# Transposing rows by DMA in a two-block spectral and attention network

## The chip, the cores and the metric

The kernel runs on one core of a Trainium2 chip. The core has a matrix engine (PE; its weight loads are shown as PEld), a vector engine (DVE), a scalar engine (ACT), a general engine (POOL) and a queue engine (SP) that issues most of the DMA transfers. The engines run their own instruction lists in order and wait for each other by semaphores. The metric is the device time of one execution in microseconds (us).

## The reference

x has 2048 rows of 512 columns in bfloat16. Four steps follow each other, each adding to x: a spectral layer, an attention layer, and both once more with the same weights.

```python
x = A_x
x = x + _A_ref(_layernorm(x, axis=-1), A_w_r, A_w_i)
x = x + _B_ref(_layernorm(x, axis=-1), B_wq, B_wk, B_wv, B_wo)
x = x + _A_ref(_layernorm(x, axis=-1), A_w_r, A_w_i)
x = x + _B_ref(_layernorm(x, axis=-1), B_wq, B_wk, B_wv, B_wo)

def _A_ref(x, w_r, w_i):          # 2-D real FFT over rows and columns, a filter, and back
    X = jnp.fft.rfft2(x.astype(jnp.float32), axes=(-2, -1)) * (w_r + 1j * w_i)
    return jnp.fft.irfft2(X, s=(S, D), axes=(-2, -1)).astype(jnp.bfloat16)

def _B_ref(x, wq, wk, wv, wo):    # 32 heads of 16; all heads share one k and one v
    q, k, v = heads(x @ wq), x @ wk, x @ wv
    p = softmax(einsum("bhqd,bkd->bhqk", q, k) * 16 ** -0.5)
    return merge(einsum("bhqk,bkd->bhqd", p, v)) @ wo
```

## The kernel before, in words

x lies in SBUF as 16 tiles of 128 rows by 512 columns (`tile_of(x_sb, k)`); `xn_sb` holds the normed rows in the same form. A matrix product on PE needs the operand that is summed over along the partitions, so x (for the spectral layer) and the normed rows (for queries, keys and values) are also kept transposed: `xT` and `xTa`, each [128, 4, 16, 128], four blocks of 128 columns for each of 16 tiles. `transpose_pair` (L191) makes two tiles of them: eight PE transposes against an identity into one bank of PSUM, and one copy to SBUF, by ACT (L198) or DVE (L200).

The spectral layer (`spectral_layer`, L210) has these stages:

- The first pass, ten steps k: transpose tiles 2k and 2k+1 of x (L195); one step later `forward` multiplies them with a cosine and sine table (L254) and ACT scales the result by the row's norm (L181); another step later `first` (L205 to L207, copied at L268) begins the transform over rows and writes to DRAM, from where `cross1` reads it in another order. Nine more steps do the same for the other half of the frequencies. `load` places the weight loads (wr_sb, wi_sb, 1 MB each) at fixed steps of the pass.
- The middle: `filtered` and `back`, with another exchange through DRAM.
- The last pass, nine steps q: `along` (L355), `last` (L368 to L370), ACT copies the sums to x (L389), DVE takes the row statistics (L152). At q = 3, 5 and 7 `norm.shift` norms tiles 0-3, 4-7 and 8-11 (two of four on ACT, L172, two on DVE, L174). At q = 4 and 6 `att.turn` transposes tiles 0-3 and 4-7 of the normed rows, and at q = 5 and 7 `att.keys_values` makes keys and values of them (L426, L452). Six idle matmuls (LASTW, L401) end the layer.

In the spectral layer the order on PE, ACT, DVE and SP is the order in the source. In attention that holds for PE and DVE; the source order is made while the kernel is built, by a planner (`Clock`, and the loop in `attention_layer`) that keeps its own account of when each engine is free. The attention layer (`attention_layer`, L589) consists of steps n. In each, PE makes a pair of score tiles (sc, L876) and ACT takes their exponential (L1042). Beside it, DVE makes a bit-arithmetic exponential of other score tiles (aux, L876, then L916, L948, and L940 on POOL), in three phases. PE multiplies both kinds with the values (L831). When there is nothing else, PE multiplies zeros (L846). Between the steps the planner places jobs: transposes of the normed tiles (`job_turn`, L621), keys and values of tiles 8-11 and 12-15, queries, and the output projection (`job_out`, L654), which adds to x (L659). A job has a first step at which it may run and a step at which it has to (`TURN` for tiles 12-15). `DVE0` is the planner's time at which DVE is free for attention's work. The transposes of tiles 8-15 (four `job_turn`) are such jobs, and the norm of tiles 12-15 is queued on DVE after the second of them.

The last four tiles' output projection of the first attention layer is left to the next spectral layer: `rest` (L1115, added to x at L1117) runs in steps k = 2 and 3 of its first pass. Large buffers come from a pool of six (`bigp`, tag "big"); a new one waits until the buffer's last reader is done.

## Time and profile before

| | us |
|---|---|
| median of 3 runs | 1414.54 (1411.57 to 1414.83) |
| the profiled execution's own time | 1409.2 |
| its span | 1407.4 |
| first spectral layer | about 0 to 92 |
| first attention layer, exponentials | 93.0 to 704 |
| second spectral layer | about 705 to 791 |
| second attention layer, exponentials | 791 to 1399 |
| ACT, exponentials (L1042), busy in all | 1218.0 |
| PE / DVE / ACT / POOL busy | 1355.2 / 1312.6 / 1337.0 / 818.2 |

Times in the profile's views are counted from the start of the span. A busy engine is not always the one that others wait for: the chain of waits follows the work that ended last back to what released it, and the rows by window tell which engine has no gap in a stage. A time in a chain row is the share of that piece in the chain, which can be shorter than the instruction.

### The profile page before, as it was taken

Reading aid. Unit: us, or ns where it says so; the run is one execution under the profiler, and the core shown is the slowest. Engines: PE = TensorE matmul, PEld = TensorE weight load, DVE = VectorE, ACT = ScalarE, POOL = GpSimd, SP = SyncE. Lnnn points to the kernel's source line nnn. Section 1 sums busy time; section 2 is a strip of 40 time slices with the busy share of each in tenths; the row PEclk is TensorE's granted clock in tenths of the full one; section 3 lists DMA queues with packets and bytes.
Section 4 is the critical chain, followed back from the end, with each engine's and each line's share of the span. In section 5 each row is a group of like instructions: output and inputs, shape, how many; then the busy total and the mean of one; then the engine's idle time right before and its main releaser. Section 6 shows DMA issues by size and latency. Waiting matters only on the chain.

```text
span 1407.4 us, 34962 instructions
## 1 busy us (share of the span) xinstructions
PE 1355.2 (96%) x14166; PEld 473.3 (34%) x14166; DVE 1312.6 (93%) x2274; ACT 1337.0 (95%) x1551; POOL 818.2 (58%) x477
## 2 busy tenths in 40 slices
PE   8899999999999999999997999999999999999998
PEld 6642232222222222222275422322222222222222
DVE  5679999999999999999966899999999999999997
ACT  6689999999999999999956899999999999999997
POOL 2115676667666667667600166666666666666665
PEclk9999999999999999999999999999999999999999
DMA  8700000000000000000064000000000000000000
GB/s 261 221 7 2 2 2 2 1 2 1 2 2 2 2 2 2 2 1 2 2 186 145 1 1 2 1 2 9 5 5 2 6 9 5 2 1 9 9 2 16
DMA packets 38242, 32.94 MB, mean 23 GB/s; under 512 B 3520, under 2 KB 35520, under 8 KB 37568
## 3 DMA queue, kind: packets, MB, share of 16 engines
q1 hardware_dynamic: 35104, 27.40, 6.7%
q8 instruction: 110, 1.80, 0.6%
q0 software_dynamic: 576, 2.10, 0.4%
q10 hardware_dynamic: 2400, 1.21, 0.3%
q14 instruction: 52, 0.43, 0.1%
HBM read 20.22 MB, written 10.49 MB: 22 GB/s over the span
## 4 chain that ended last, share of the span: by engine, by line
ACT 49%; PE 33%; issue 8%; DVE 6%; DMA 2%; POOL 0%; SPq 0%; DVEq 0%; ACTq 0%
ACT e L1042 47%; PE pv L831 13%; PE sc L876 11%; DVE ph L916 2%; PE aux L876 2%; PE ps L254 2%; DVE ln_stats L152 1%; PE aux L426 1%; PE ps L205 1%; PE aux L654 1%; PE pv L846 1%; DMA tab_C<-const_C 1%; DVE ph L948 1%; DMA B<-D 1%; PE ps L355 1%
## 5 line engine op out<-in xcount | busy, mean ns | idle before, releaser
L1042 ACT ACTIVATE e<-sc 128x1024 bf16<-128x1024 f32 x1328 | 1218.0, 1175 | 1.9 <-PE sc L876 1.9
L940 POOL TENSOR_TENSOR ph<-ph,step 128x1024 int32<-128x1024 int32 x404 | 763.2, 1892 | 410.3 <-DVE ph L948 284.3
L916 DVE TENSOR_SCALAR ph<-aux 128x512 uint16<-128x512 f32 x1440 | 903.3, 678 | 19.9 <-PE aux L876 15.8
L831 PE MATMUL pv<-ph,vaug 128*32 128x512 bf16 x4320 | 548.8, 386 | 0.6 <-POOL ph L940 0.3
L876 PE MATMUL sc<-QT,Kv 32*128 32x512 bf16 x2656 | 522.0, 380 | 19.1 <-ACT e L1042 13.9
L831 PE MATMUL pv<-e,vaug 128*32 128x512 bf16 x2656 | 483.9, 384 | 0.3 <-ACT e L1042 0.3
L876 PE MATMUL aux<-QT,Kv 32*128 32x512 bf16 x1440 | 455.9, 384 | 0.0
L876 PEld LDWEIGHTS <-Kv 32*128 32x128 bf16 x4096 | 183.0, 91 | 525.9 <-issue 517.8
L846 PE MATMUL pv<-wo_sb,zeros 128*32 128x512 bf16 x1200 | 257.8, 383 | 0.0
L831 PEld LDWEIGHTS <-vaug 128*32 128x32 bf16 x6976 | 147.5, 94 | 292.6 <-issue 281.6
L948 DVE TENSOR_SCALAR ph<-ph 128x2048 uint16<-128x2048 uint16 x316 | 216.1, 684 | 0.5
L158 POOL TENSOR_TENSOR ln_rstd<-ln_veps,mhalf 128x4 f32<-128x4 f32 x16 | 16.6, 1036 | 140.1 <-DVE ln_veps L157 140.0
L152 DVE BATCH_NORM_STATS2 ln_stats<-x_sb 128x6 f32<-128x512 bf16 x64 | 43.4, 678 | 22.1 <-ACT x_sb L389 16.3
L846 PEld LDWEIGHTS <-zeros 128*32 128x32 bf16 x1200 | 60.2, 94 | 1.9 <-issue 0.3
L746 DVE STREAM_TRANSPOSE oT<-pv 128x512 f32<-128x512 f32 x64 | 45.1, 705 | 9.2 <-PE pv L831 9.2
L181 ACT ACTIVATE Pk<-ps,ln_rstd 128x256 bf16<-128x256 f32 x64 | 27.1, 478 | 15.9 <-PE ps L254 15.6
L426 PE MATMUL aux<-xTa,wq_sb 128*128 128x512 bf16 x120 | 39.5, 385 | 0.4 <-DVE ph L916 0.2
L254 PE MATMUL ps<-tab_PH,xT 128*128 128x256 bf16 x256 | 35.5, 286 | 1.6 <-DVE xT L200 1.0
L268 DVE CAST A<-ps 128x512 bf16<-128x512 f32 x28 | 19.3, 690 | 18.8 <-PE ps L207 18.8
L654 PE MATMUL aux<-wo_sb,ph 128*128 128x512 bf16 x96 | 31.8, 384 | 1.5 <-DVE ph L916 1.0
L768 POOL TENSOR_TENSOR on<-oT,rden 128x512 bf16<-128x512 f32 x30 | 31.7, 1058 | 2.0 <-DVE rden L772 1.8
L254 PEld LDWEIGHTS <-xT 128*128 128x128 bf16 x256 | 24.8, 102 | 5.5 <-DVE xT L200 1.3
(108 smaller groups left out, 677.9 us busy)
## 6 DMA issues: line engine op xcount, KB each, us to landing
D<-A SPq DMA_DIRECT2D x32, 128.0 KB, 3.3
A<-D SPq DMA_DIRECT2D x16, 256.0 KB, 3.5
D<-B SPq DMA_DIRECT2D x32, 128.0 KB, 3.2
B<-D SPq DMA_DIRECT2D x12, 256.0 KB, 4.1
tab_H<-const_H POOLq DMA_DIRECT2D x4, 512.0 KB, 6.3
wr_sb<-in_A_w_r_dram SPq DMA_DIRECT2D x2, 1024.0 KB, 6.1
wi_sb<-in_A_w_i_dram SPq DMA_DIRECT2D x2, 1024.0 KB, 7.5
out_dram<-x_sb SPq DMA_DIRECT2D x15, 128.0 KB, 1.7
```

Of the source, the lines that this page charges most:

```text
L152: nc.vector.bn_stats(st, src)
L254: nc.tensor.matmul(ps[:, j, :], lhsT=xT[:, cc, 2 * k + j, :], rhs=PH[:, cc, 256 * h:256 * h + 256], start=(cc == 0), stop=(cc == NC - 1), ...
L426: self.nc.tensor.matmul(ps, lhsT=w(c), rhs=self.xTq[:, c, qc * 512:(qc + 1) * 512], start=(c == 0), stop=(c == NC - 1), skip_group_check=True)
L654: nc.tensor.matmul(ps, lhsT=OTs[qb][:, g4, kk * P:(kk + 1) * P], rhs=wo_sb[:, g4, :], start=first, stop=last, skip_group_check=True)
L746: end = clock.now(clock.FLIP, lambda: nc.vector.transpose(out=oT[:, par].rearrange("p b c -> p (b c)"), in_=pv), clock.last + clock.MM_END)
L831: nc.tensor.matmul(pv_tiles[gi][32 * i:32 * i + 32, :], lhsT=vaug[:, kc, j, :], rhs=es, start=((gi, i) not in started), stop=(left[gi, i] ...
L846: nc.tensor.matmul(pv_tiles[gi][32 * i:32 * i + 32, :], lhsT=att.zeros, rhs=wo_sb[:, 0, :], start=False, stop=False, skip_group_check=True)
L876: nc.tensor.matmul(out, lhsT=Kv[r, par, kc * P:(kc + 1) * P], rhs=QT[r, g, qb * 512:(qb + 1) * 512], start=True, stop=True, skip_group_che ...
L916: end = clock.now(clock.Z, lambda: nc.vector.tensor_scalar(out=z.bitcast(U16), in0=ps, scalar1=SCALE * LOG2E * 128.0, scalar2=127.0 * 128. ...
L940: nc.gpsimd.tensor_tensor(out=copy.bitcast(I32), in0=z.bitcast(I32), in1=step.to_broadcast([P, w // 2]), op=ALU.add)
L948: nc.vector.tensor_scalar(out=one.bitcast(U16), in0=z.bitcast(U16), scalar1=float(PHASE[1]), scalar2=None, op0=ALU.add)
L1042: nc.scalar.activation(out=e[:, 0:ng * 512], in_=sc[:, 0:ng, :].rearrange("p a b -> p (a b)"), func=ACT.Exp, scale=SCALE)
```

## The change: DMA transposes

A new function issues one DMA transpose on SP for one tile, SBUF to SBUF:

```diff
+def turn_tile(nc, rows, xT, k):
+    nc.sync.dma_start_transpose(out=xT[:, :, k, :], in_=tile_of(rows, k))
```

All 16 tiles of normed rows in both layers go through it. Tiles 0-11 are transposed in the spectral layer's last pass, each group of four right after its norm (q = 3, 5, 7). Tiles 12-15 are normed at the head of attention and transposed there. The four `job_turn` are gone.

```diff
@@ last pass of spectral_layer
             if 0 <= g < 3 and odd == 0:
                 norm.shift(4 * g, (1, 3))
-            if 0 <= g < 2 and odd == 1:
-                att.turn(psum, g, "pa")
+                att.turn(g)
@@ Attention.turn
-        for k2 in (2 * qc, 2 * qc + 1):
-            transpose_pair(self.nc, self.tabs["ident"], psum, self.xn_sb, self.xT, k2, k2 % 2 == 1, tag)
+        for k in range(4 * qc, 4 * qc + 4):
+            turn_tile(self.nc, self.xn_sb, self.xT, k)
@@ attention_layer
-        def job_turn(k2):
...
+        def turn_last():
+            for k in range(12, 16):
+                turn_tile(nc, att.xn_sb, att.xT, k)
+
+        clock.later(0.2, lambda: norm_in.bias(12))
+        for i in range(4):
+            clock.later(clock.one(2), lambda i=i: norm_in.one(12, i, False), True)
+        clock.later(0, turn_last)
+        while clock.queue:
+            clock.flush_one()
...
-        jobs = [(0, 0, job_turn(4)), (0, 0, job_turn(5)), (0, 0, job_keys(2)), (0, 0, job_values(2)),
-                (TURN, TURN, job_turn(6)), (TURN, TURN, job_turn(7)), (TURN, TURN, job_keys(3)), (TURN, TURN, job_values(3))]
+        jobs = [(0, 0, job_keys(2)), (0, 0, job_values(2)), (TURN, TURN, job_keys(3)), (TURN, TURN, job_values(3))]
@@ constants
-TURN, DVE0 = 7, 1.7
+TURN, DVE0 = 12, 2.4
```

For the second spectral layer, x is transposed during the first attention layer: once twelve tiles have their sums and the last queries are made, which frees the buffer of `xTa`, SP issues twelve transposes; the last four tiles follow in `rest`. The second layer's first pass has no PE transposes of x; the first layer's keeps them.

```diff
+        xT, summed = [], [0]
+
+        def turn_sums():
+            if store is None and summed[0] == 12 and ("Q", NQB - 1, 3) in made:
+                xT.append(att.bigp.tile([P, NC, 16, P], BF, name="xT", tag="big"))
+                for t in range(12):
+                    turn_tile(nc, x_sb, xT[0], t)
@@ spectral_layer
-        xT = bigp.tile([P, NC, 16, P], BF, name="xT", tag="big")
+        xT = feed.xT or bigp.tile([P, NC, 16, P], BF, name="xT", tag="big")
...
-            if k < 8:
+            if k < 8 and feed.xT is None:
                 transpose_pair(nc, tabs["ident"], psum, x_sb, xT, k, feed.busy or k % 2 == 1, "pa")
@@ rest
                 nc.vector.tensor_tensor(out=tile_of(x_sb, t), in0=ps, in1=tile_of(x_sb, t), op=ALU.add)
+                turn_tile(nc, x_sb, xT[0], t)
                 norm_out.stats(t, tile_of(x_sb, t))
```

More of the change, by code (lines that the diff above doesn't have):

```diff
@@ L429, in project, with turn @@
                 yield
-    def turn(self, psum, qc, tag):
+    def turn(self, qc):
         if qc == 0:
@@ L619, in job_queries @@
             made.add(("Q", qc, g))
-        def job_turn(k2):
-            while k2 > 5 and ("N", 3) not in made:
-                clock.flush_one()
-            ps = aux_tile((P, 2, NC, P), BF)
-            for tt in range(2):
-                for cc in range(NC):
-                    nc.tensor.transpose(ps[:, tt, cc, :], tile_of(att.xn_sb, 2 * k2 + tt)[:, cc * P:(cc + 1) * P],
-                                        att.tabs["ident"])
-                if tt == 0:
-                    yield
-            dst = att.xT[:, :, 2 * k2:2 * k2 + 2, :].rearrange("d c tt p -> d tt c p")
-            evict(clock.CAST, lambda: nc.vector.tensor_copy(out=dst, in_=ps))
-            if k2 == 5:
-                clock.later(0.2, lambda: norm_in.bias(12))
-                for i in range(4):
-                    clock.later(clock.one(2), lambda i=i: norm_in.one(12, i, False), True)
-                clock.later(0, lambda: made.add(("N", 3)))
+            turn_sums()
+        def turn_last():
[7 more added lines that the diff above has]
+            clock.flush_one()
         def job_keys(qc):
@@ L671, in job_out @@
                 return
+            summed[0] += 1
+            turn_sums()
             clock.later(0.96, lambda: norm_out.stats(k, tile_of(x_sb, k)))
@@ L1117, in rest @@
                 nc.vector.tensor_tensor(out=tile_of(x_sb, t), in0=ps, in1=tile_of(x_sb, t), op=ALU.add)
+                turn_tile(nc, x_sb, xT[0], t)
                 norm_out.stats(t, tile_of(x_sb, t))
-    rest.busy = False
+    rest.busy, rest.xT = False, xT[0]
     return rest
@@ L1185, in feed @@
             nc.vector.tensor_single_scalar(out=tabs["S1N"][:, part], in_=tabs["S1"][:, part], scalar=-1.0, op=ALU.mult)
-    feed.busy = True
+    feed.busy, feed.xT = True, None
     for layer in range(2):
```

## Prediction

> **What bounds the kernel now.** I read the page's totals first, then a table of windows, the chain of waits around the stages that the change touches, and the DMA rows.

> Window table (start:end, length, then busy us and instruction count of PE, PEld, DVE, ACT, POOL; granted clock, DMA share, GB/s):
> ```profile
> 84.00:91.00 7.00, 7.00 (x62) 4.04 (x61) 4.93 (x13) 5.14 (x9) 1.01 (x1) 1.00 0.00 0
> 96.00:106.00 10.00, 9.77 (x107) 4.23 (x105) 9.96 (x22) 9.75 (x11) 1.89 (x1) 1.00 0.00 0
> 200.00:300.00 100.00, 98.28 (x1043) 29.55 (x1039) 96.81 (x164) 100.00 (x110) 67.27 (x37) 1.00 0.01 2
> 721.00:736.00 15.00, 14.76 (x158) 13.14 (x156) 7.72 (x12) 9.73 (x23) 0.00 (x0) 1.00 0.89 226
> ```
> In attention ACT does nothing but the exponentials (L1042), is busy 100.00 of 100 us, and starts 109 in 100 us (one per 0.917; the count takes in one at an edge). Its rows in part 5 show 1.9 us of idle time before all 1328. So attention lasts 664 x 0.917 us after its first exponential: fewer PE or DVE instructions there gain next to nothing, and an early wait of ACT is not made up. What can move is when attention's exponentials get going, and the spectral stages, where PE fills the windows (7.00 of 7.00; 14.76 of 15.00).

> The chain of waits (start, length, work), end of the first spectral stage and start of attention:
> ```profile
> 73.96 1.52 ACT xn_sb L172 x2
> ...
> 79.41 1.02 PE ps L426 x4
> ...
> 84.29 0.89 PE pst L195 x16
> ...
> 89.49 1.52 ACT xn_sb L172 x2
> ...
> 95.30 0.59 PE aux L426 x2
> 95.89 0.34 PE sc L876 x2
> 96.25 1.94 ACT e L1042 x2
> ```
> Rows 0 to 3 are normed at 73.9 to 75.5, their keys begin at 79.41; the last of rows 8 to 11 is ready at 91.0, their keys begin at 95.30. The exponentials began at 93.04, had a gap of 0.36, and never stop after 96.25.

> The same chain, start of the second spectral stage:
> ```profile
> 706.17 0.70 DVE xT L200
> 706.92 1.05 PE ps L254 x8
> 707.97 0.88 PE ps L1115 x4
> ...
> 717.71 1.05 PE ps L254 x8
> ...
> 719.20 0.45 PE pst L195 x8
> ```
> A group of eight PE transposes takes 0.45 of PE; twice PE waits for a copy of xT.

> DMA rows (KB each, median us from issue to landing) and SP's queue (start, length of the issue):
> ```profile
> D<-A SPq DMA_DIRECT2D x32, 128.0 KB, 3.3
> D<-B SPq DMA_DIRECT2D x32, 128.0 KB, 3.2
> wr_sb<-in_A_w_r_dram SPq DMA_DIRECT2D x2, 1024.0 KB, 6.1
> out_dram<-x_sb SPq DMA_DIRECT2D x15, 128.0 KB, 1.7
> ```
> ```profile
> 43.36 1.24 SPq L132 DMA_DIRECT2D tab_CS<-const_CS  x1
> 44.65 0.43 SPq L132 DMA_DIRECT2D tab_PSC<-const_PSC  x1
> ```

> **The price that no row shows.** A DMA transpose of one tile (128x512, 128 KB) is not in this trace. Two numbers matter: p, the time that SP holds for one issue, and L, from issue to landing. For p the ends are 0.43 (a plain issue) and 1.24 (the longest single one). For L they are 1.7 and 4.1 (B<-D, 256 KB). A transpose cuts the tile into 256-byte runs, twice as many as D<-A's 512-byte ones, so more must be set up than for a plain copy: I take p = 1.24, the upper end, and L = 3.2, the median of a plain 128 KB. All are on SP, one after another.

> **End of each spectral stage (twice).** Removed: 32 PE transposes in att.turn (two groups of 16, 0.89 each on PE), two ACT copies (1.02) and two DVE copies (0.69). Added: 12 DMA transposes on SP, behind plain loads that landed before (wq, wo issued by 65). Nothing else is on SP here.
> Rows 0 to 3: the first is ready at 74.3, so the fourth issue is at 74.3 + 3 x 1.24 = 78.0 and lands at 81.2. PE without its 0.89, and ACT without a copy of 1.02, would be at the keys by 78.4; instead it waits until about 81.25: 1.85 later than before, not 1.0 earlier. Behind that wait stand, in PE's order, the values, the first queries and all following sums.
> Rows 4 to 7: ready by about 81, landed by 87; their keys stand at 81.25 + (87.62 - 79.41 - 0.89) = 88.6. Hidden, with 1.5 us to spare.
> Rows 8 to 11: their norm hangs on the sums before the second keys. Before, the first came 2.2 after the start of these keys (87.62 to 89.8), so now 90.8. The fourth issue is at 90.8 + 3.72 = 94.5, landing 97.7. Before, PE transposed these rows inside attention, behind one pair of scores each; now the second thing PE does in attention, after the first pair, is the keys of rows 8 to 11. PE gets there at 88.6 + 1.27 (keys, values) + 2.15 (ten sums) + 1.3 (LASTW) + 0.3 = 93.6 and waits 4.1 us. The second pair of scores is queued behind. From keys to the next exponential it took 0.95 (95.30 to 96.25); now exponential 2 starts at 98.65, and the fourth, which was at 96.25, at 98.65 + 2 x 0.907 = 100.5. **Loss: 4.2 us per layer, 8.4 in all.**
> With both ends: at p = 0.43, L = 1.7 the keys start at 78.4 (PE and ACT decide), 85.7 and 91.0, and the same exponential at 93.75: a gain of 2.5 per layer. At p = 1.24, L = 4.1 it is a loss of 6.0.

> **Attention.** Four groups of 8 PE transposes and four DVE copies (0.68) per layer go; ACT is the bound, so zero, and it stays covered as ACT is at 100%. The norm of rows 12 to 15 (bias, four of 0.35) moves to DVE's head of attention, behind POOL's rstd (L158, 1.01). Queued behind it are the krep copy and all vector units; rstd comes about 96.8, the norm ends at 98.4, and the first copy behind it needs the keys of 97.7 and after: zero, and 1.5 us if rstd were late. Rows 12 to 15 are wanted at step 12 (TURN), about 98.65 + 11 x 0.917 - 1 = 107.7; their fourth lands by 97.4 + 3.72 + 3.2 = 104.3: zero, cover 3.4 us. The twelve transposes of x can begin when the last queries (651) and sums (637) of attention 1 are made and are wanted at 705: 12 x 1.24 + 3.2 = 18 of 53 us, zero. Exponentials, vector units and POOL copies stay 1328, 1440 and 404; zero-fillers on PE rise by 51, in gaps.

> **Start of the second spectral stage (once).** Removed: 64 PE transposes, four ACT copies, four DVE copies. The first copy (0.70 at 706.17) stands on DVE ahead of the OT transposes that the rest of the output projection (L1115) waits for: 0.85 earlier. Six groups inside the PE-filled loop: 6 x 0.45 = 2.7. The wait before 717.71: 0.56. Sum 4.1. Against it: rows 12 to 15 of x are added there (L1117) and transposed by SP. 12 and 13 go at once; 14 and 15 are issued after the 1 MB of wr_sb, issue near 712.1 and landing 6.1 later, 718.2; I put them at 719.2, and the forward step that reads them would start at 722.72 - 4.1 = 718.6: 0.6 lost. **Gain 3.5.** Ends: 4.4 (no such wait) and 2.0 (L = 4.1 and DMA, busy 0.89 until 736, giving some back); all later steps of that stage follow PE.

> **Sum.** 8.4 - 3.5 = +4.9 us on the profiled execution (1409.2 with a span of 1407.4): 1414.1. The runs shown have a median 5.3 above that execution, so 1414.54 + 4.9 = 1419.4. Range of this case: L = 2.2 with gain 3.5 gives +0.9 (2 x 2.2 - 3.5), L = 4.1 with gain 2.0 gives +10.

> [...] For a 128x128 transpose the row is 0.45 per eight on PE plus a copy of 0.68 for the pair of tiles. [...]

> **Rivals.**
> 1. Faster: an issue is as cheap as a plain one. Place: the fourth transpose before the keys of rows 0 to 3 and 8 to 11. p = 0.43 with L = 3.2 gives keys at 79.0, 86.3 and 93.1, a gain of 0.4 per layer, total -4.3 (1410.2); with L = 1.7, 2 x -2.5 and -4.4 give -9.4 (1405.1). For it: most issues of the trace take 0.43 to 0.5. Against: none of them transposes. At L = 3.2 it decides at p = 0.85, where the sum is zero.
> 2. Transfers do not overlap: each tile takes its 3.2 alone. Then the twelfth lands at 74.3 + 12 x 3.2 = 112.7, the keys of rows 8 to 11 are 17.4 later, exponentials 19 per layer: +38 - 2 = +36 (1450). Against: plain DMAs of 128 KB issue 0.5 apart and overlap in the rows. [...]
> 3. PE's clock falls in the wait of 4.1 us. Eight L254 matmuls took 1.91 at 14.47 and 1.04 at 17.22, so PE does start slow; after the gap of 2.17 before 745.00 it did not. At half pace a step of 0.917, 98% PE, takes about 1.8; four us so lose 2 per layer: +4.9 + 4 = +9 (1423). [...]

> **Chances.** Forecast 0.55; rival 1 0.24; rival 2 0.08; rival 3 0.13. Within 0.3% (4.2 us, about what a measurement can tell from no change): 0.25 of the forecast, as +0.9 to +4.2 lies in its range, and 0.05 of rival 1: 0.30. Faster 0.19, rounded to 0.20. Slower 0.50: 0.30 of the forecast and rivals 2 and 3. Eight in ten: from rival 1's lower end, 1405, to 1430 (rival 3 at L = 4.1: +10 + 4, and a margin of 1.5); rival 2 is left out.

> **What would show it.** SP rows of the transposes: length 1.24, landing 3.2. PE waits before the keys of about 2.8 and 4.1 us per layer, released by DMA. ACT idle of some 4 us after its first exponential, then one per 0.917. The forward step of x rows 14 and 15 some 3.5 earlier after the end of attention 1. Wrong: if p is below 0.85, if the keys wait for ACT or DVE rather than a DMA, or if exponentials run at another pace than 0.917.

## The result, and the profile after

The changed kernel takes 1430.43 us (median of 5 runs, 1428.15 to 1435.57); the kernel before took 1414.54 beside it (5 runs, 1411.57 to 1415.77). The ratio is 1.0122, 95% interval 1.0098 to 1.0146: slower by 16 us where +4.9 was forecast, with an upper end of 1430. The profiled execution of the changed kernel took 1435.57 (span 1433.8), the slowest of its five, and that of before 1409.2, its fastest, so the two traces lie 26.4 apart. 5.0 of that is there before any changed instruction has run: rows 0 to 3 are normed by 80.49 instead of 75.48 behind the same first passes. In the profiles of kernels whose first pass is the same, this point lies between 75.0 and 81.2. Losses are therefore counted from the end of that norm in each layer.

Windows of the profile after, for the stages that the prediction showed (columns as there):
```profile
84.00:91.00 7.00, 4.90 (x32) 2.53 (x34) 2.60 (x9) 3.28 (x5) 0.56 (x1) 0.76 0.57 77
103.00:113.00 10.00, 9.47 (x69) 2.19 (x69) 6.17 (x14) 6.86 (x7) 0.00 (x0) 0.57 0.27 54
200.00:300.00 100.00, 96.14 (x1042) 28.69 (x1043) 98.12 (x166) 100.00 (x111) 67.09 (x37) 1.00 0.01 1
726.00:741.00 15.00, 14.09 (x138) 11.74 (x136) 9.96 (x19) 7.57 (x19) 1.04 (x1) 1.00 0.82 187
```
The granted clock was 1.00 in all four stages before. It is 0.76 at the end of the spectral stage (its last pass, called the tail below) and 0.57 in the first steps of attention (called the head), where PE is busy 9.47 of 10 us but does 69 matmuls where it did 107 in the ten microseconds shown of before, and ACT is busy only 6.86. In the middle of attention nothing has changed: ACT is full.

The chain of waits there (start, length, work):
```profile
78.97 1.52 ACT xn_sb L172 x2
...
83.37 2.43 DMA xTa<-xn_sb
85.89 1.02 PE ps L429 x4
86.91 0.39 PE ps L455 x16
87.29 1.63 PE ps L429 x4
...
100.30 0.74 ACT e L1048
101.04 2.45 DMA xTa<-xn_sb
103.53 0.60 PE aux L429 x2
104.14 0.32 PE sc L882 x2
104.46 0.97 PE aux L429 x2
105.43 0.54 PE sc L882 x2
```
A transfer now stands ahead of the keys of rows 0 to 3 (85.89) and of rows 8 to 11 (103.53); PE waits 3.18 and 3.32 us for them, and ACT, behind the second, 3.17:
```profile
85.89 1.02 PE L429 MATMUL ps<-xTa,wka 128*128 128x512 bf16 x4 [3.18 <-DMA xTa<-xn_sb]
...
103.53 0.60 PE L429 MATMUL aux<-xTa,wka 128*128 128x512 bf16 x2 [3.32 <-DMA xTa<-xn_sb]
```
```profile
104.50 1.02 ACT L1048 ACTIVATE e<-sc 128x1024 bf16<-128x1024 f32 x1 [3.17 <-PE sc L882]
```
In the second layer PE waits 3.20 and 3.71 and ACT 4.19. Behind both waits the same work takes longer: the four projections of the queries 1.63 (0.88 in the chain before, at 80.82), a pair of scores 0.54 (0.34 before, at 95.89).

The DMA rows (KB where given, median us to landing) and the transposes in the tile's rows (length of the issue in ns, least, median, most):
```profile
xTa<-xn_sb SPq DMA_TRANSPOSE x32, 2.4
xT<-x_sb SPq DMA_TRANSPOSE x16, 2.5
```
```profile
L204 SPq DMA_TRANSPOSE xTa<-xn_sb x16: 1190/1218/1639, 79.4 to 107.2; - x16
```
So p is 1.22 and L 2.4.

SP's queue at the start of the second spectral stage:
```profile
727.96 0.58 SPq L235 DMA_DIRECT2D wr_sb<-in_A_w_r_dram  x1
728.64 4.34 SPq L204 DMA_TRANSPOSE xT<-x_sb  x2
```
The last two tiles of x stand behind the 1 MB load, as forecast. The first of their two issues took 3.03 and landed 6.19 after its start; the second took 1.22, as usual, and the rest of the 4.34 is a pause between them.

And a gap that the forecast had not: near the 257th exponential of the first layer, PE's and DVE's rows show
```profile
339.95 1.21 DVE L157 TENSOR_SCALAR ln_veps<-ln_mv 128x4 f32<-128x4 f32 x1
```
```profile
341.80 0.40 PE L837 MATMUL pv<-ph,vaug 128*32 128x512 bf16 x4 [0.89 <-DVE ph L922]
```
In the kernel before, the same row statistic stands at the same place (325.11) and takes 0.17. Here it takes 1.21, and beside it on POOL stands
```profile
339.24 1.89 POOL L946 TENSOR_TENSOR ph<-ph,step 128x1024 int32<-128x1024 int32 x1 [1.10 <-PE aux L882]
```
That instruction ends at 341.13 and the row statistic at 341.16. In the changed order of attention the two fall together; PE misses 1.41 of two microseconds, its clock falls to 0.50 until 350, and the exponentials lose 3.3 us. With normed rows only, the same place loses 2.1, with 3.4 us at half clock (337.6 to 341.0); with all three mended it loses about 1.2, with the clock at 1.00 from 325 to 340. So most of it is the clock.

### The profile page after: what moved, and what is told of

The parts are those of the page before. It is cut to its first block, busy times and chain, and to the rows that moved or that the text cites. A ratio compares the mean times of both kernels' runs of the same rounds, so it can differ in the third digit from the quotient of the medians.

```text
span 1433.8 us, 34679 instructions
## 1 busy us (share of the span) xinstructions
PE 1353.2 (94%) x13958; PEld 466.8 (33%) x14025; DVE 1308.6 (91%) x2258; ACT 1333.2 (93%) x1543; POOL 816.9 (57%) x477
## 3 DMA queue, kind: packets, MB, share of 16 engines
q10 hardware_dynamic: 2400, 1.21, 0.3%
## 4 chain that ended last, share of the span: by engine, by line
ACT 42%; PE 38%; DVE 8%; issue 8%; DMA 3%; SPq 0%; POOL 0%; DVEq 0%; ACTq 0%
ACT e L1048 41%; PE pv L837 15%; PE sc L882 12%; DVE ph L922 4%; PE ps L258 2%; PE aux L882 2%; DVE ph L954 1%; PE aux L429 1%; PE ps L209 1%; DVE ln_stats L152 1%; DMA D<-B 1%; DMA xTa<-xn_sb 1%; DMA x_sb<-in_A_x_dram 1%; PE pv L852 1%; DMA D<-A 1%
## 5 line engine op out<-in xcount | busy, mean ns | idle before, releaser
L837 PE MATMUL pv<-ph,vaug 128*32 128x512 bf16 x4320 | 556.8, 387 | 1.3 <-DVE ph L922 0.9
L837 PE MATMUL pv<-e,vaug 128*32 128x512 bf16 x2656 | 498.6, 387 | 0.3 <-ACT e L1048 0.3
L852 PE MATMUL pv<-wo_sb,zeros 128*32 128x512 bf16 x1271 | 268.0, 388 | 0.0
L158 POOL TENSOR_TENSOR ln_rstd<-ln_veps,mhalf 128x4 f32<-128x4 f32 x16 | 16.5, 1031 | 151.7 <-DVE ln_veps L157 141.0
L429 PE MATMUL aux<-xTa,wq_sb 128*128 128x512 bf16 x90 | 32.4, 385 | 2.5 <-issue 1.6
L316 ACT CAST X<-ps 128x512 bf16<-128x512 f32 x32 | 17.4, 613 | 11.5 <-issue 6.5
## 6 DMA issues: line engine op xcount, KB each, us to landing
D<-A SPq DMA_DIRECT2D x32, 128.0 KB, 3.5
D<-B SPq DMA_DIRECT2D x32, 128.0 KB, 2.9
wr_sb<-in_A_w_r_dram SPq DMA_DIRECT2D x2, 1024.0 KB, 7.1
wi_sb<-in_A_w_i_dram SPq DMA_DIRECT2D x2, 1024.0 KB, 6.7
out_dram<-x_sb SPq DMA_DIRECT2D x15, 128.0 KB, 1.7
```

Of the source, the lines that this page charges most:

```text
L429: self.nc.tensor.matmul(ps, lhsT=w(c), rhs=self.xTq[:, c, qc * 512:(qc + 1) * 512], start=(c == 0), stop=(c == NC - 1), skip_group_check=True)
L837: nc.tensor.matmul(pv_tiles[gi][32 * i:32 * i + 32, :], lhsT=vaug[:, kc, j, :], rhs=es, start=((gi, i) not in started), stop=(left[gi, i] ...
L852: nc.tensor.matmul(pv_tiles[gi][32 * i:32 * i + 32, :], lhsT=att.zeros, rhs=wo_sb[:, 0, :], start=False, stop=False, skip_group_check=True)
```

## The experiments

Theories. **A**: the loss lies in the normed rows alone, at the keys of rows 0 to 3 and 8 to 11, and x brings nothing, as the exchange through DRAM takes PE's saving back. **B**: x brings the forecast 3.5. **C**: x is part of the loss. Within A, **A1**: half of the loss is PE's clock, which falls in the waits; **A2**: it is the waits alone.

Most runs are read with one measure: from the end of the norm of rows 0 to 3 to an early exponential of the same number in both kernels, once they follow each other without gaps, minus the same in the kernel before. For the changed kernel, layer 1, tenth exponential: (114.83 - 80.49) - (96.25 + 6 x 0.917 - 75.48) = 34.34 - 26.27 = 8.1 us.

| kernel | median us, beside before | ratio (95%) | loss at the head, layer 1 / 2 |
|---|---|---|---|
| changed | 1430.43, 1414.54 | 1.0122 (1.0098 to 1.0146) | 8.1 / 8.1 |
| normed rows only | 1429.91, 1412.38 | 1.0124 (1.0101 to 1.0147) | 7.9 / 8.0 |
| x only | 1415.57, 1412.38 | 1.0017 (1.0002 to 1.0033) | none |
| idle matmuls in the waits | 1424.69, 1412.38 | 1.0089 (1.0058 to 1.0120) | 3.4 / 3.5 |
| four tiles in one | 1424.86, 1415.11 | 1.0076 (1.0059 to 1.0093) | 4.4 / 3.7 |
| all three mended | 1416.49, 1412.81 | 1.0038 (1.0021 to 1.0054) | 0.0 / 0.1 |
| rows 0 to 7 only, keys later | 1420.56, 1415.11 | 1.0048 (1.0030 to 1.0067) | -0.5 / 4.1 |
| rows 0 to 7 only, four in one | 1413.07, 1415.49 | 0.9980 (0.9965 to 0.9994) | -1.7 / -1.6 |

### Which part costs: normed rows alone, x alone

In the first, x is transposed on PE again; the second is the kernel before with only x's transposes by DMA.
```diff
@@ normed rows only: the changed kernel
-            turn_sums()
...
-                turn_tile(nc, x_sb, xT[0], t)
-    rest.busy, rest.xT = False, xT[0]
+    rest.busy, rest.xT = False, None
@@ x only: the kernel before
+                turn_tile(nc, x_sb, xT[0], t)
-    rest.busy = False
+    rest.busy, rest.xT = False, xT[0]
```

> The changed kernel, but x of the second spectral layer goes back to PE transposes; only the normed rows go by DMA. Theory A (the loss of 16 us lies in the normed rows alone: 2 us per layer at the keys of rows 0-3, 6 at the keys of rows 8-11, and the transposes of x bring nothing because the exchange through DRAM eats their gain): +14 to +18 over the kernel before. Theory B (the transposes of x bring the 3.5 us of the prediction): +18 to +21. Theory C (the transposes of x are a part of the loss): under +12.

> The kernel before, with only x of the second spectral layer by DMA transposes, those of the normed rows on PE as before. Theory A: -1 to +2 us against the kernel before, PE at the end of the first pass some 4 us earlier, but the first matmul of the second half of the filter (A against tab_G after its wait for DMA) no earlier. Theory B: -3 to -4.5. Theory C: +4 or more.

Normed rows alone cost 17.5 us, x alone 3.2 in medians (1.0017, so 0.3 to 4.7). As far as these runs can tell, the loss is in the normed rows, and the gain of 3.5 on x does not show: B falls. Theory A missed x alone too (-1 to +2 expected): x may cost a little, and the upper end of the interval reaches C's +4.

### Where PE's saving on x went

Two more kernels with x alone. In one, SP's two 1 MB loads come later; in the other, PE gets back about as many matmuls in the second pass as its transposes took.
```diff
@@ later loads
-            if k == 3:
+            if k == 5:
                 nc.sync.dma_start(out=wr_sb, ...
-            elif k == 6:
+            elif k == 10:
                 nc.sync.dma_start(out=wi_sb, ...
@@ idle matmuls in the pass
+            if k < 8 and feed.xT is not None:
+                pad = psum.tile([P, 512], F32, name="ps", tag="pa")
+                for _ in range(4):
+                    nc.tensor.matmul(pad, lhsT=ident, rhs=tabs["PSC"][:, 0, :], start=True, stop=True, skip_group_check=True)
```

> The kernel before, with only x turned by DMA, and with the two loads of spectral weights of 1 MB each moved later on SP's queue: the first from the fourth step of the pass to the sixth (behind the transposes of tiles 12 to 15), the second from the seventh to the eleventh. Theory A (the time that PE saves is given back because the writes to D wait on SP's queue behind transposes and behind the loads' traffic): most of the gain comes back, 1411 to 1413, against 1415.6 without the move. Rival E (the exchange lasts as long whatever stands before it, or the weights now come too late for the filter): 1414 to 1418.

> The kernel before, with only x turned by DMA, and with four idle matmuls of 128x512 in each of the eight steps of the second spectral stage in which the kernel before transposed on PE: about as much PE time as the transposes took, 7 us in all; nothing uses what they compute. Theory A (the exchange over D on the DMA engines and SP's queue sets the end of the pass, so PE's saving there was worth nothing): no change against x alone, 1414 to 1417. Theory B (PE's saving was worth its 3 to 4 us, and something else took it back): 1418 to 1422.

Later loads: 1420.62 beside 1415.11 (1.0046, 1.0031 to 1.0061), worse than x alone. The move also acts in the first layer, and the second load now goes out just ahead of the last reads. Both ranges are missed (A 1411 to 1413, E 1414 to 1418); so this does not show that the loads' place took the gain back. Its profiled run was granted 0.992 of the full clock over 1419.2 us, or 22.7 us at half pace (0.995 over 1414.7 with x alone, 14.1); no run took that apart. Idle matmuls: 1414.93 beside 1415.49 (1.0002, 0.9992 to 1.0012), no change, as theory A has it. PE spent the time: in the 35 us after the end of attention it was busy 33.88, against 29.5 with x alone. The last reads of the exchange on SP, before, x alone, x with idle matmuls (the first attention ends at 704.2, 709.8 and 707.1):
```profile
739.91 1.62 SPq L272 DMA_DIRECT2D A<-D  x2
```
```profile
744.25 2.60 SPq L276 DMA_DIRECT2D A<-D  x2
```
```profile
742.66 2.59 SPq L276 DMA_DIRECT2D A<-D  x2
```
They end 37.3, 37.0 and 38.1 us after the end of attention. DVE's last copy of the pass, which follows PE, ends 32.4, 28.9 and 34.4 after it: 3.5 earlier with x alone and 2.0 later with idle matmuls than before, while the reads come 0.3 earlier and 0.8 later. The filter behind them needs these reads. So the exchange sets the end of this pass, and less work for PE showed no gain there; what inside the exchange bounds it was not separated (with x alone the DMA share is 0.50 to 1.16 in its windows of 5 us, and SP's writes and reads wait in order).

### What sets the waits: half tiles, four tiles, later keys

```diff
@@ half tiles
-    nc.sync.dma_start_transpose(out=xT[:, :, k, :], in_=tile_of(rows, k))
+    for h in range(2):
+        nc.sync.dma_start_transpose(out=xT[:, 2 * h:2 * h + 2, k, :], in_=tile_of(rows, k)[:, 256 * h:256 * h + 256])
@@ four tiles in one (xT kept tile by tile: [128, 16, 4, 128])
-        for k in range(4 * qc, 4 * qc + 4):
-            turn_tile(self.nc, self.xn_sb, self.xT, k)
+        turn_four(self.nc, self.xn_sb, self.xT, qc)
@@ later keys
-        jobs = [(0, 0, job_keys(2)), (0, 0, job_values(2)), ...
+        jobs = [(5, 5, job_keys(2)), (5, 5, job_values(2)), ...
```

> The changed kernel, with each transpose of a tile made by two instructions of half a tile. Theory A1 with an issue priced by the instruction: eight issues of 1.2 us for four tiles, the keys of rows 0-3 and of rows 8-11 begin 4.9 us later, the keys of rows 4-7 wait too (about 3 us), and the time grows by 10 to 25 us from 1430, to 1440 to 1455. Rival (issue priced by its blocks, 0.6 us for half a tile): 1428 to 1434.

> The changed kernel, with the four tiles of normed rows of a group turned by one transpose on SP's queue instead of four (16 blocks in one instruction; the transposed rows lie tile by tile instead of column by column). Theory A1 (the keys of rows 0-3 and 8-11 wait because SP issues four transposes one after the other, 1.22 us each, and the clock falls in that wait): if one issue is priced by the instruction (1.2 to 1.6 us), the chain from the last normed tile to the keys shrinks from 5.4 us to about 4, both waits of 3.2 and 3.3 us shrink to 1.5 to 2, and the time falls by 2 to 8 us from 1430, to 1422 to 1428. Rival (the issue is priced by its blocks, four times 1.22 for one of four tiles, and it can only begin once all four tiles are normed): both waits grow by 1 us or stay, 1429 to 1434.

> The changed kernel with the jobs for keys and values of rows 8-11 put at step 5 of attention instead of step 0, so that five pairs of scores and zero-fillers stand ahead of the matmul that waits for the DMA. Theory A: the 6 us per layer at the head of attention go, so +3 to +6 over the kernel before instead of +16, ACT idle under 1 us there. Rival (the loss sits in the spectral layer's end, or the wait only moves to step 5): +12 to +16.

Half tiles: 1453.74 beside 1415.11 (1.0275, 1.0254 to 1.0296). The time is in A1's range (1440 to 1455). An issue of half a tile takes 1.24 us, as long as one of a whole tile. PE's first wait:
```profile
89.44 2.12 PE L430 MATMUL ps<-xTa,wka 128*128 128x512 bf16 x4 [7.05 <-DMA xTa<-xn_sb]
```
7.05 for 3.18 is 3.9 more; the four extra issues of 1.24 would make 5.0. Four tiles in one: one issue of 1.70 to 2.06, landing 4.2 us after its start; PE waits less in both places,
```profile
84.15 1.02 PE L433 MATMUL ps<-xTa,wka 128*128 128x512 bf16 x4 [2.20 <-DMA xTa<-xn_sb]
...
99.15 0.64 PE L433 MATMUL aux<-xTa,wka 128*128 128x512 bf16 x2 [2.36 <-DMA xTa<-xn_sb]
```
and the time falls to 1424.86 (expected 1422 to 1428). The waits were to be 1.5 to 2 and the issue 1.2 to 1.6, so the size has some part in the price. Here (1.24 for half a tile, 1.22 for one, 1.70 to 2.06 for four) an issue is priced mostly by the instruction, and the number of issues sets most of the waits. Windows of the same kernel (start:end, length, PE, clock, DMA share, GB/s):
```profile
85.00:90.00 5.00, 4.95 (x42) 1.00 0.58 108
...
102.00:104.00 2.00, 2.00 (x27) 0.50 1.09 206
```
After the wait of 2.20 in the tail the clock stays full; after 2.36 at the head it still halves.

Later keys: 1428.92 beside 1412.38 (1.0119, 1.0090 to 1.0147), nothing clear gained: +16.5, outside theory A's +3 to +6 and just above the rival's +12 to +16. The wait for the transfer at the head is gone and the heads lose 5.4 and 6.6 in place of 8.1; the wait in the tail stays (3.21), with its halved clock. But the scores of rows 8 to 11, and later those of rows 12 to 15, then wait for the masked keys,
```profile
107.66 0.39 PE L882 MATMUL sc<-QT,Kv 32*128 32x512 bf16 x1 [0.86 <-DVE Kv L449]
...
118.01 0.39 PE L882 MATMUL sc<-QT,Kv 32*128 32x512 bf16 x2 [1.04 <-DVE Kv L449]
```
and the clock is 0.85 and 0.81 from 105 to 115. Keys that are wanted at once cannot simply be put back.

### The clock by itself

Fourteen matmuls that nothing uses stand in PE's list ahead of the keys of rows 0 to 3 and of rows 8 to 11. The wait for the transfer stays; PE is not idle in it.
```diff
@@ idle matmuls in the waits: ahead of both projections of keys
+            for _ in range(14 if qc == 2 else 0):
+                nc.tensor.matmul(ps, lhsT=att.tabs["ident"], rhs=att.tabs["PSC"][:, 0, :], start=True, stop=True,
+                                 skip_group_check=True)
```

> The changed kernel with 14 idle 128x512 matmuls (3.0 us at full clock) on PE ahead of the keys of rows 0-3 and of rows 8-11, in the time in which PE waits for the transposes anyway. Theory A1 (half of the loss is PE's clock, which falls in the wait and stays at half for 3 to 11 us): clock 1.00 behind both waits, +7 to +11 over the kernel before instead of +16. Theory A2 (the wait alone costs, the clock follows but hides behind ACT): +14 to +17.

The clock is 1.00 behind both waits in both layers, and after one gap the exponentials run on; windows of the head (start:end, length, PE, clock, DMA share, GB/s) and ACT's rows:
```profile
95.00:100.00 5.00, 4.76 (x22) 1.00 0.39 79
100.00:105.00 5.00, 4.92 (x60) 1.00 0.62 83
```
```profile
95.96 1.02 ACT L1054 ACTIVATE e<-sc 128x1024 bf16<-128x1024 f32 x1 [0.59 <-PE sc L888]
100.14 10.19 ACT L1054 ACTIVATE e<-sc 128x1024 bf16<-128x1024 f32 x11 [3.16 <-PE sc L888]
```
The loss at the head falls from 8.1 to 3.4 and 3.5 us per layer, though the wait is as long as before. So of 8.1, 3.4 is waiting and 4.7 the clock: by this measure and the clock A1 holds and A2 falls. The median does not decide it: it falls by less than the 9.3 that both layers would make, from +16 to +17.5 to +12.3, between A1's +7 to +11 and A2's +14 to +17. In this profile the second spectral stage loses another 3.1 us; the mean clock of the whole profiled run is 0.996 over 1420.8, some 11 us at half pace, and no run took that apart.

### All of it together

Four tiles in one transpose, the keys of rows 0 to 3 one step later in the tail, and ten idle matmuls ahead of the keys of rows 8 to 11.
```diff
-            if 0 <= g - 1 < 2 and odd == 0:
+            if (g - 1, odd) in ((0, 1), (1, 0)):
                 att.keys_values(psum, g - 1, "pa")
```

> The changed kernel with its planner constants (12 and 2.4), four tiles in one transpose, the keys of rows 0 to 3 one step later, and ten idle matmuls of 128x512 (nothing uses them) in the wait for rows 8 to 11 to hold the clock. Theory A1 (waits and the clock that falls in them make up the loss): against the 1424.9 of the four-in-one transposes alone, the wait of 2.2 us before the keys of rows 0 to 3 goes and the half clock of 10 us at each layer's head goes, 2 x 2 and 2 x 1.5 to 2.5 us: 1415 to 1420. Rival (something else in the transposes costs): 1421 to 1426.

1416.49 beside 1412.81. Nothing is lost at the heads any more (0.0 and 0.1), the clock is 1.00 in all windows from 80 to 114, ACT's gaps there are short,
```profile
91.77 1.02 ACT L1052 ACTIVATE e<-sc 128x1024 bf16<-128x1024 f32 x1 [1.30 <-PE sc L886]
...
94.74 5.61 ACT L1052 ACTIVATE e<-sc 128x1024 bf16<-128x1024 f32 x6 [1.95 <-PE sc L886]
```
and the gap near the 257th exponential is 0.76 long, without a fall of the clock. The waits and the clock make up most of the loss: of +16 to +17.5, 3.7 is left. No run took that apart; in this trace about 1.2 of it goes near the 257th exponential and 1.3 in the second spectral stage.

### The changed order of attention

The change also moves two constants of the planner. One kernel with normed rows only, and one with all three mends, had both back at their old values; another with normed rows only had just DVE0 back.
```diff
@@ normed rows, old plan; and all three mended, old plan
-TURN, DVE0 = 12, 2.4
+TURN, DVE0 = 7, 1.7
@@ normed rows, old DVE0
-TURN, DVE0 = 12, 2.4
+TURN, DVE0 = 12, 1.7
```

> The changed kernel without the part on x (x is turned by PE as before), and with the planner's two constants back at 7 and 1.7. Theory A1 with the dip: the changed order of the attention's jobs, not the transposes, makes the gap of about 3 us near the 257th exponential of the first layer; with the old constants that gap is gone and the time falls by 1.5 to 3 us against 1429.9, to 1426 to 1429. Rival (the gap comes from the removed evictions of the transposes, whatever the constants are): the gap stays, 1429 to 1432.

> The changed kernel with each cause that theory A1 names taken away: four tiles in one transpose, the keys of rows 0 to 3 one step later, ten idle matmuls of 128x512 (nothing uses them) in the wait for rows 8 to 11 to hold the clock, and the planner's constants back at 7 and 1.7. Theory A1 (waits at the head of the attention, the clock that falls in them, and the gap from the changed order make up the loss): 1415 to 1420, against 1430. Rival (the transposes cost something else, such as their traffic beside other work): 1422 to 1430.

> The changed kernel without the part on x, and with only the second planner constant back, 1.7 for 2.4 (the first stays 12). If the gap near the 257th exponential of the first layer comes from the work that the second constant moves, it goes, and the time falls by 1 to 3 us against the 1429.9 of the normed rows alone: 1426.5 to 1429. If it comes from the jobs that the transposes no longer take, the gap stays, and the time with it: 1429 to 1432.

1449.52 beside 1415.49 (1.0235, 1.0213 to 1.0256), 1428.93 (1.0099, 1.0079 to 1.0119) and 1445.95 beside 1412.81 (1.0238, 1.0219 to 1.0258). The first and last fell outside everything expected; the middle one is in its rival's range, for a reason that is not the rival's. The 3 us gap near the 257th exponential does go (0.6 is left in each), but a worse one comes. In the last of the three, DVE's second mask of the keys of rows 12 to 15 slips behind some 10 us of vector units, and PE waits for it:
```profile
131.96 1.67 DVE L449 TENSOR_SCALAR Kv<-krep,tab_hmask 128x512 bf16<-128x512 bf16 x1
```
```profile
133.69 0.60 PE L879 MATMUL sc<-QT,Kv 32*128 32x512 bf16 x2 [2.96 <-DVE Kv L449]
```
The first mask ran at 120.69, 11.3 us earlier; in normed rows only, with 2.4, the two are 3.5 apart. That first mask took 0.34, the second 1.67; what held the second was not shown. The clock is 0.50 for the 12 us that follow, and the second layer's exponentials have the same gaps. So the second constant could not go back as it was; that this is because DVE has the norm of rows 12 to 15 at its head is an argument, not shown. The gap at the 257th exponential is the price of the order found with the new constants. It was not taken away alone.

### Part of the change

In the kernel before, only rows 0 to 7 by DMA; rows 8 to 15, x and the planner stay. First tile by tile, with both groups' keys a step later; then four tiles in one, with only the keys of rows 0 to 3 a step later.
```diff
@@ both, in the last pass of the spectral layer
-            if 0 <= g < 2 and odd == 1:
+            if 0 <= g < 2 and odd == 0:
                 att.turn(psum, g, "pa")
@@ first
-            if 0 <= g - 1 < 2 and odd == 0:
+            if 0 <= g - 1 < 2 and odd == 1:
@@ second
-            if 0 <= g - 1 < 2 and odd == 0:
+            if (g - 1, odd) in ((0, 1), (1, 0)):
```

> The kernel before, with only the normed rows 0 to 7 of each layer turned by DMA, and their keys and values one step later in the spectral stage's tail, where PE still has sums to make; rows 8 to 15, x and the planner's constants stay as before. Theory A1 (the loss of the change is PE's wait for the transposes and the clock that falls in it, not the transposes themselves): PE is spared the 1.09 and 0.89 us of transposes per layer, waits 1 us or less, keeps its full clock, and the time falls by 2 to 5 us, to 1407 to 1410. Rival W (keys and values that come later make the first scores later by as much, or the transposes hold up other transfers of SP): 1411 to 1418.

> The kernel before, with only the normed rows 0 to 7 of each layer turned by DMA, four tiles in one transpose, with the keys and values of rows 0 to 3 one step later in the tail and those of rows 4 to 7 at their old place; everything else is as before. Theory A1 (only waits and the clock cost): PE is spared about 2 us of transposes per layer, waits 0.6 us at most, keeps its full clock, and the time is 1 to 4 us below the kernel before. Rival W (PE's tail is not what the first exponential waits for, or the clock falls again): 0 to 5 us above it.

The first is slower, 1420.56, against A1's 1407 to 1410 and above W's 1411 to 1418 too. The values of rows 4 to 7 now come last, and the first scores wait for DVE's copy of them, in layer 1 and in layer 2:
```profile
94.40 0.39 PE L880 MATMUL sc<-QT,Kv 32*128 32x512 bf16 x2 [1.66 <-DVE vaug L464]
...
796.26 0.39 PE L880 MATMUL sc<-QT,Kv 32*128 32x512 bf16 x2 [1.76 <-DVE vaug L464]
```
After the first the clock stays full; after the second it is 0.50 from 800 to 808 and the head loses 4.1. The second kernel has 0.86 us of wait in the tail at most, a clock of 1.00, and each layer's exponentials start 1.6 to 1.7 earlier: 1413.07 beside 1415.49, ratio 0.9980 (0.9965 to 0.9994). It is the only version that beats both kernels. Its gain, 2.4 us in medians (0.8 to 5.0 by the ratio), lies below the 3.3 that both layers' exponentials come earlier; per layer the tail is spared about 2 us of PE transposes.

## Why the prediction was right and wrong

- **p and L.** p = 1.24 was right (1.22), but not for its reason. The 256-byte runs are there (512 packets of 256 bytes for each transpose in the trace after), but more to set up because of them would make half a tile cheaper and four tiles four times as dear; they cost 1.24 and 1.7 to 2.06. The value was luck. L was taken at 3.2 and is 2.4.
- **End of the spectral stage, rows 0 to 3.** From the norm's end to the keys, 5.8 us were forecast (75.5 to 81.25) and 5.4 measured (80.49 to 85.89). The issues on SP made the wait, as said. Rows 4 to 7 were hidden, as said.
- **Rows 8 to 11.** PE was to wait 4.1 us and waited 3.32 in layer 1 and 3.71 in layer 2; ACT idle of some 4 us after the first exponential was 3.17 and 4.19.
- **"Loss: 4.2 us per layer, 8.4 in all" is the step that failed.** For the waits alone it was slightly high: 3.4 and 3.5. But the forecast let PE run at full clock behind them. The clock halved and cost another 4.7 per layer; 8.1 per layer, 16.2 in all, was measured. Rival 3 had the halved clock and too small a size and chance: half pace for 4 us, 2 per layer; the 4 us were the author's estimate, and no run shows them. It was 0.59 and then 0.50 from 104 to 114, 10.2 us in all, while PE had more to do in each step than half its pace allows (98.28 of 100 us at full clock before), and it fell in the tail too (0.66 in 86 to 90). Windows (start:end, length, PE, clock, DMA share, GB/s):
```profile
86.00:90.00 4.00, 4.00 (x29) 0.66 0.72 80
...
106.00:114.00 8.00, 8.00 (x69) 0.50 0.23 47
```
The trace before held a sign of this: its clock is halved from 57.45 to 60.86, behind 3.4 us in which PE was busy only a third of the time. Rival 3 looked at two other places.
- **Attention: zero.** Pace (0.917), and the cover of rows 12 to 15, held. But the planner made another order, in which a row statistic on DVE took 1.21 in place of 0.17, and a gap that cost 3.3 us came with it in this trace. The term was put at nothing by counting instructions; a changed order needs a price of its own.
- **Start of the second spectral stage: gain 3.5.** The transposes were hidden, tiles 14 and 15 stood behind wr_sb, and PE was through its pass sooner. Yet "all later steps of that stage follow PE" was wrong: the last reads of the exchange come 37 to 38 us after attention with or without PE's work. No gain showed.
- **Rival 1** fell with p. **Rival 2** fell too, as transfers overlap: issues that start 1.3 apart each land 2.4 after their start.
- **Direction** was right for the right reason, PE waiting for SP's issues; the size was not. The measured time lies just past the range's upper end, 1430, which came from rival 3 and not from the forecast's own sum.

## What to carry to other kernels

Cost a DMA transpose by its issue: here 1.2 us of the queue for half a tile or a whole one and under 2.1 for four tiles, so put as much as possible in one instruction and its reader a step later, where PE still has work. When a change makes PE wait for about 2 us or longer at a point after which PE is nearly full, price the halved clock behind it as well; waits of 1.76 to 3.7 us halved the clock here, though not each time (2.20 did not), and at the head it cost more than the wait. And look for what ends a stage before crediting an engine with saved time: PE was 98% busy in the second first pass, and less work for it there showed no gain.
